# Attention with a computed position bias and a gated MLP on one core: another order of the bias groups, with three attention steps among the last ones

## The chip, the cores and the metric

The kernel runs on one core of one Trainium2 chip. The metric is device time in microseconds (us) of one execution; lower is better. The engines are TensorE (PE in the profile; PEld is its weight load), VectorE (DVE), ScalarE (ACT), GpSimd (POOL) and SyncE (SP), which here only issues transfers. Each works through its own instructions in the order in which the program emits them, and waits on semaphores for the others.

## What is computed

Attention over 4 batches, 8 heads, 576 positions and 64 dimensions per head, with a bias on the scores that a small network makes from the distance of two positions; then, on the 2304 resulting rows, a product with `w_in`, a rational function, and a product with `w_out`.

```python
psi_rel = np.log1p(np.abs(pos[:, None] - pos[None, :]))
psi_i = np.log1p(np.maximum(pos[:, None], 1.0))
h = np.maximum((psi_rel / psi_i)[..., None] @ w1 + b1, 0.0)
scores = scale * q @ k.T + (h @ w2).transpose(2, 0, 1)[None]
attn = softmax(scores); x = attn @ v
h = x @ w_in
P = a[0] + a[1] * h + a[2] * h**2 + a[3] * h**3
Q = 1.0 + abs(b[0]) * abs(h) + abs(b[1]) * h**2
out = (P / (Q + 1e-6)) @ w_out
```

## The kernel before

The program has three parts, and the change lies in the first and in the seam to the second.

**Bias groups** (L564 to L655). The bias of a row of positions depends on the distance alone, so it is made as tables in DRAM. There are 36 groups `n` of 16 positions. For a group, `relu(n)` (L596) makes four rows of hidden units, each as long as the largest distance that occurs, `dist(n)` (576 elements for the first and the last group, 304 in the middle); VectorE makes them, and in every fourth group ScalarE makes one of the four (`ENG`, L587). They go into a ring of 14 slots, and run `LEAD` = 2 groups ahead. Four products on TensorE (L633) make the group's tile `pb` in PSUM, ScalarE evicts it in two instructions (L642) into one of five tiles `e`, and SP writes `e` to the table in DRAM (L647). Table `tab[g]` holds eight groups, the last one four. The loop goes over `n` in rising order, so the tables are finished in the order 0 to 4.

`load_bias(p, c)` (L242) loads table `c` for the pair of heads `p` into SBUF as three transfers (288, 256 and 32 KB; two of 144 KB for table 4). For the first pair it stands in the loop, two groups after a table is done; that of table 4 comes after the loop (L655).

**Attention** (L320 to L562). Sixteen units (a pair of heads, a batch) of five steps make 80 steps; step `c` of a unit takes 128 queries of both heads, step 4 the last 64 of both. `step_a(i)` (L495) emits, in this order: transfers for later steps; the score products of step `i` (L340); the rest of the exponentials of step `i - 1`; the transposes of step `i - 2` (L418) and their copies; some products with `v` (L451, L456); then on VectorE the reduction of step `i` (L351), which adds bias table `c` of the unit's pair and takes the row maximum, and the first exponential (L369) on ScalarE. A step's scores lie in one or two tiles of the PSUM pool `ps_sc`, which has two, so the scores of a step wait until the reduction of an earlier one has read its tile. The tiles `pb` come from the same pool. The transposes use two tiles of the pool `ps_tp`. The last `EARLY` = 2 groups have steps 0 and 1 among them (L653); the other steps follow after L655.

**Weight jobs.** The weights of the second part are split into two halves by 20 jobs in the background of attention: two loads of 512 KB (`wx`, `wy`, L127 and L128), five VectorE and one ScalarE instructions, two stores. `run_jobs` (L486), called at the end of a step, emits as many of their VectorE instructions as `JOB_OPS` says (1, 2, 2, 1, 1 by the step), and every transfer that comes before the next of them. With 0, as in step 2, it emits the loads of the first two jobs alone; from step 3 on the first job's VectorE instructions follow.

SP issues nearly all transfers on one queue, in the order emitted. Before the bias groups, a prologue on VectorE (L576 to L586) scales the constants; ScalarE's row uses the table `pts` that it leaves.

The lines that set the seam:

```python
if k == 2 and g:
    load_bias(0, g - 1)
if n >= NG - EARLY:
    step_a(n - NG + EARLY)
...
load_bias(0, 4)
```

Of the kernel before, what the change touches and what calls it, by code (L numbers as in the profile page):

```python
# [16 lines left out]
P = 128  # L17
# [17 lines left out]
def tile_attn_moe(  # L35
# [185 lines left out]
    with tc.manual_schedule():  # L221
# [3 lines left out]
        with ExitStack() as actx:  # L225
# [260 lines left out]
            def run_jobs(n):  # L486
                while bg and (n > 0 or bg[0][0] != "dve"):
                    kind, fn = bg.pop(0)
                    if kind == "act":
                        actq.append(fn)  # L490
                    else:
                        fn()
                    n -= kind == "dve"

            def step_a(i):  # L495
                def ok(d):
                    return 0 <= i - d < NS

                if i < NS:
                    u, c = steps[i]  # L500
                    if c == 1 and u + 1 < NU:
                        load_qk(u + 1)
                    if c == 2 and u + 1 < NU:
                        load_v(u + 1)
                    g = {(0, 4): 0, (1, 1): 1, (1, 4): 2, (2, 1): 3, (2, 4): 4}.get((units[u][1], c))
                    if g is not None and units[u][0] + 1 < NP:
                        load_bias(units[u][0] + 1, g)
                    if i == NS - 7:
                        load_x(0, 0)
                first = []  # L510
                if NS - 4 <= i < NS:
                    first = split_x(0, i - NS + 4)
                if first:
                    first[0]()
                    later.append(first[1])
                while len(later) > (1 if i < NS - 1 else 0):
                    later.pop(0)()
                if ok(0):
                    e_qk(i)
                if ok(1):  # L520
                    for j in heads(i - 1)[1:]:
                        e_exp(i - 1, j)
                run_act()
                if ok(TL):
                    hs = heads(i - TL)
                    for j in hs:
                        for o, x in e_tp(i - TL, j):
                            A.copy(out=o, in_=x)  # L528
                    tails, fin = e_tail(i - TL)
                for _ in range(PV_KEYS[(i - TL) % 5] if i < NS + TL else len(fill)):  # L530
                    if fill:
                        e_pv(*fill.pop(0))
                if ok(0):
                    for j in heads(i):
                        e_ttr(i, j)
                    e_exp(i, heads(i)[0])
                if ok(1) and steps[i - 1][1] == 4:
                    e_recip(steps[i - 1][0])
                if ok(TL):
                    for o, x in tails:  # L540
                        A.copy(out=o, in_=x)
                    if fin:
                        fin()
                    u2, c2 = steps[i - TL]
                    if c2 in (1, 4):
                        fill.extend((u2, c2 // 4, kc) for kc in range(5))
                if 0 <= i - NS < 2:
                    mm1(0, i - NS)
                if i == NS:
                    w_carve(3)  # L550
                    w_load(KH - 2, 0)
                    w_load(KH - 1, 0)
                if i == NS + 1:
                    load_x(1, 1)
                u2, c2 = divmod(i - TL, 5)
                if c2 == 0 and 1 < u2 <= NU:
                    e_norm(u2 - 2)
                if c2 == 0 and 0 < u2 <= NU:
                    load_rb(u2 - 1)
                if i >= 2:  # L560
                    run_jobs(JOB_OPS[c2] if i >= 3 else 0)
                e_pvout()  # L562

            with ExitStack() as bctx:  # L564
# [8 lines left out]
                nc.sync.dma_start(out=lts, in_=ltab)  # L573
                nc.scalar.dma_start(out=cs, in_=cst)
                load_qk(0, nc.scalar)
                V.tensor_scalar(out=lts, in0=lts, scalar1=w1s, scalar2=None, op0=ALU.mult)  # L576
                V.tensor_scalar(out=pts, in0=pts, scalar1=b1s, scalar2=None, op0=ALU.mult)
                V.tensor_scalar(out=nts, in0=pts, scalar1=-1.0, scalar2=None, op0=ALU.mult)
                V.tensor_scalar(out=w28, in0=cs[:, 8 + 5 * NG:], scalar1=8.0, scalar2=None, op0=ALU.mult)
                V.memset(qc, 1.0 + 1e-6)  # L580
                V.memset(wmin, -8.0 * 0x38000000)
                pc = ps_tp.tile([P, 512], F32, tag="tp", name="pc")
                T.matmul(pc[:, 0:1], w28, b1s, start=True, stop=True)
                V.memset(c8, 0.0)
                V.tensor_copy(out=c8[:, 0:1], in_=pc[:, 0:1])
                V.tensor_copy(out=c8[0:96, 1:2], in_=pc[0:96, 0:1])  # L586
                ENG = ["DDDA" if n % 4 == 0 else "DDDD" for n in range(NG)]  # L587

                def dist(n):
                    return max(NROW * n + NROW, S - NROW * n)  # L590

                rows = {}
                LEAD, EARLY = 2, 2
                nring = [0]

                def relu(n):  # L596
                    for c, e in enumerate(ENG[n]):
                        r = ring[nring[0] % len(ring)][:, :dist(n)]
                        nring[0] += 1
                        m = 4 * n + c  # L600
                        if e == "A":
                            A.activation(out=r, in_=lts[:, :dist(n)], func=AF.Relu, bias=pts[:, m:m + 1])
                        else:
                            V.tensor_scalar(
                                out=r, in0=lts[:, :dist(n)], scalar1=nts[:, m:m + 1], scalar2=None,
                                op0=ALU.max,
                            )
                        rows[n, c] = r
# [9 lines left out]
                    after[15 + f] = [lambda f=f: [w_load(f, z) for z in range(2)]]  # L618
                bg = in_order(bg, after)

                for n in range(LEAD):
                    relu(n)
                for n in range(NG):
                    if n == 4:
                        load_v(0)
                    if n + LEAD < NG:
                        relu(n + LEAD)
                    ps = ps_sc.tile([P, 2, 512], F32, tag="sc", name=f"pb{n}")
                    ps = ps.rearrange("p a s -> p (a s)")
                    for s0 in range(0, dist(n), 512):  # L630
                        s1 = min(s0 + 512, dist(n))
                        for c in range(4):
# [15 lines left out]
                        out=tab[g][NROW * k:NROW * k + NROW, :, x0:x0 + EW].rearrange("r h x -> (r h) x"),  # L648
                        in_=e,
                    )  # L650
                    if k == 2 and g:
                        load_bias(0, g - 1)
                    if n >= NG - EARLY:  # L653
                        step_a(n - NG + EARLY)
                load_bias(0, 4)  # L655
                A.activation(out=babs, in_=abs_[:, 4:6], func=AF.Abs)

            wpool = ctx.enter_context(
# [273 lines left out]
```

## Time and profile before

| | |
|---|---|
| median of 3 runs | 746.05 us (744.64 to 746.75) |
| the profiled execution | 745.69 us |
| its span, from the first to the last instruction | 743.9 us |
| TensorE busy | 723.1 us (97%) |
| VectorE, ScalarE, GpSimd busy | 581.7 us (78%), 514.9 us (69%), 184.5 us (25%) |

The profile comes from one execution. Times in it are microseconds from the first instruction, names are those of the program with the number of the buffer left out, and the line is that of the kernel. A busy time includes the overlap of pipelined instructions; idle time is put down to what released the engine. TensorE's clock has two levels, 2.4 GHz (1.00 in the windows) and 1.2 GHz (0.50).

### The profile page before, as it was taken

The page shows a single profiled execution, that of the slowest core. Times are in us where ns is not written, and L with a number is a line of the kernel's source. Part 1 is how long each engine was busy: PE and PEld are TensorE (multiplying, and loading weights), DVE is VectorE, ACT ScalarE, POOL GpSimd, SP SyncE. Part 2 cuts the span into 40 slices and gives each one's busy share as a digit, 9 for nine tenths or more (in the row PEclk, how much of TensorE's full clock was granted, in tenths as well). Part 3 has the DMA queues.
Part 4 walks back from the last instruction along what each step waited for, and adds up shares of the span by engine and source line. Part 5 has one row for each costly group of instructions (what it writes and reads, how often), then busy time and mean ns, then how long its engine had stood idle before and what let it go on. Part 6 is the DMA issues. An engine that isn't in the chain of part 4 may idle for free.

```text
span 743.9 us, 12201 instructions
## 1 busy us (share of the span) xinstructions
PE 723.1 (97%) x4210; PEld 550.7 (74%) x4210; DVE 581.7 (78%) x979; ACT 514.9 (69%) x965; POOL 184.5 (25%) x106
## 2 busy tenths in 40 slices
PE   6898999999999999999999999999999999999997
PEld 2235666665666666668889989998899989998896
DVE  7995566666676667546999999999997869787766
ACT  5987788887888787877575766667675665556552
POOL 0000000000000000003444445454554345434442
PEclk9999999999999999999999999999999999999999
DMA  4878797788988899637433344547952123031121
GB/s 140 300 285 279 237 291 268 224 269 285 317 261 284 271 283 297 206 89 236 153 128 127 128 151 140 172 166 240 306 185 85 54 75 126 3 128 47 39 86 42
DMA packets 107421, 137.67 MB, mean 185 GB/s; under 512 B 17104, under 2 KB 66528, under 8 KB 107360
## 3 DMA queue, kind: packets, MB, share of 16 engines
q1 hardware_dynamic: 106768, 136.11, 55.9%
q8 instruction: 33, 0.54, 0.3%
q10 hardware_dynamic: 592, 0.78, 0.3%
q14 instruction: 28, 0.23, 0.1%
HBM read 94.96 MB, written 41.90 MB: 184 GB/s over the span
## 4 chain that ended last, share of the span: by engine, by line
PE 86%; DMA 5%; DVE 3%; SPq 2%; ACT 2%; issue 1%; POOL 0%; DVEq 0%; ACTq 0%; POOLq 0%
PE o L767 25%; PE h L315 24%; PE sc L340 11%; PE pv L451 9%; PE tp L418 9%; PE pb L633 4%; PE pv L456 3%; DMA wy<-in_w_in_dram 2%; ACT e L642 2%; DMA wy<-in_w_out_dram 1%; PE pv L433 1%; DMA k<-in_kt_dram 1%; DMA tab<-e 1%; DMA cst<-in_cst_dram 0%; DVE m L722 0%
## 5 line engine op out<-in xcount | busy, mean ns | idle before, releaser
L697 POOL TENSOR_TENSOR u<-u,w 128x768 f32<-128x768 f32 x48 | 96.7, 2015 | 475.2 <-DMA xr<-xd 338.6
L351 DVE CUSTOM_DVE_ANT_0 s<-sc,bias 128x576 f32<-128x576 f32 x144 | 104.0, 755 | 76.4 <-PE sc L340 74.1
L369 ACT ACTIVATE p<-s,m 128x576 f32<-128x576 f32 x144 | 113.2, 786 | 3.4 <-DVE m L351 3.1
L528 ACT COPY ptm<-tp 128x512 f32<-128x512 f32 x144 | 78.2, 588 | 52.6 <-PE tp L418 52.0
L694 ACT ACTIVATE w<-h 128x768 f32<-128x768 f32 x48 | 39.0, 813 | 101.6 <-PE h L315 99.0
L736 POOL TENSOR_TENSOR gl<-m,r 128x768 fp32r<-128x768 f32 x47 | 87.1, 1854 | 72.5 <-DVE m L729 72.5
L315 PE MATMUL h<-xh,wg 128*128 128x384 f32 x384 | 101.8, 336 | 0.0
L340 PE MATMUL sc<-k,q 64*128 64x288 f32 x512 | 82.6, 430 | 4.3 <-DVE m L351 2.6
L418 PEld LDWEIGHTS tp<-ident,p 128*128 128x128 f32 x576 | 63.1, 141 | 26.7 <-issue 11.5
L451 PE MATMUL pv<-ptm,v 128*64 128x320 f32 (+1 forms) x512 | 80.4, 425 | 0.0
L418 PE MATMUL tp<-ident,p 128*128 128x128 f32 x576 | 79.8, 280 | 0.0
L767 PE MATMUL o<-wg,gh 128*128 128x512 f32 x288 | 79.0, 391 | 0.0
L340 PEld LDWEIGHTS sc<-k,q 64*128 64x128 f32 x512 | 45.7, 187 | 37.3 <-issue 7.9
L701 ACT ACTIVATE r<-u,qc 128x768 f32<-128x768 f32 x48 | 45.1, 940 | 37.5 <-POOL u L697 37.3
L315 PEld LDWEIGHTS h<-xh,wg 128*128 128x128 f32 x384 | 69.7, 188 | 1.1
L722 DVE SCALAR_TENSOR_TENSOR m<-u,qc,gh 128x768 f32<-128x768 f32 x48 | 66.0, 1375 | 5.4 <-DVE gh L715 0.5
L705 DVE TENSOR_TENSOR t<-t,h 128x768 f32<-128x768 f32 x48 | 45.5, 948 | 26.7 <-ACT t L696 15.8
L315 PE MATMUL h<-xh,wih 128*128 128x384 f32 x192 | 65.0, 338 | 0.9 <-DVE t L708 0.9
L315 PE MATMUL h<-xl,wih 128*128 128x384 f32 x192 | 64.7, 337 | 0.2 <-DVE xl L301 0.2
L315 PE MATMUL h<-xh,wil 128*128 128x384 f32 x192 | 64.7, 337 | 0.0
L315 PE MATMUL h<-xl,wg 128*128 128x384 f32 x192 | 64.4, 335 | 0.0
L715 DVE SCALAR_TENSOR_TENSOR gh<-t,cst,r 128x768 fp32r<-128x768 f32 x48 | 56.5, 1176 | 8.2 <-ACT r L702 5.8
(77 smaller groups left out, 1343.4 us busy)
## 6 DMA issues: line engine op xcount, KB each, us to landing
tab<-e SPq DMA_DIRECT2D x36, 295.5 KB, 3.5
wx<-in_w_in_dram SPq DMA_DIRECT2D x16, 512.0 KB, 5.5
wy<-in_w_in_dram SPq DMA_DIRECT2D x16, 512.0 KB, 6.0
wx<-in_w_out_dram SPq DMA_DIRECT2D x16, 512.0 KB, 4.7
wy<-in_w_out_dram SPq DMA_DIRECT2D x16, 512.0 KB, 5.7
ws<-wh SPq DMA_DIRECT2D x32, 256.0 KB, 5.6
ws<-wl SPq DMA_DIRECT2D x32, 256.0 KB, 4.8
wg<-ws SPq DMA_DIRECT2D x32, 256.0 KB, 5.3
```

Of the source, the lines that this page charges most:

```text
L315: T.matmul(hps[s][:, j, :TT], w[:, k, sl], x[:, k, :], start=(k == 0 and z == 0), stop=(k == KD - 1 and z == 2),)
L340: T.matmul(sc[i, j][:, a, :SH], l, k[r, o + a * SH:o + (a + 1) * SH], start=True, stop=True,)
L351: V.tensor_tensor_reduce(out=t.rearrange("p (a s) -> p a s", a=2), in0=sc.pop((i, j))[:, :, :SH], in1=bias[p][:, idx, :].rearrange("p (a s ...
L369: A.activation(out=prob[i][:, z * S:z * S + S], in_=t, func=AF.Exp, bias=m, scale=-1.0, accum_out=ssum[u][:, k:k + 1],)
L418: T.transpose(ps[:, kc, :], prob[i][:, k0:k0 + P], ident)
L451: T.matmul(ps[64 * j:64 * j + 64, :w], v[:, kc, 64 * j:64 * j + 64], ptm[u, hf][:, kc, j, :w], start=(kc == 0), stop=False,)
L528: A.copy(out=o, in_=x)
L697: G.tensor_tensor(out=u, in0=u, in1=w, op=ALU.mult)
L715: V.scalar_tensor_tensor(out=hi, in0=rt[s, "t"], scalar=abs_[:, 0:1], in1=rt[s, "r0"], op0=ALU.add, op1=ALU.mult,)
L722: V.scalar_tensor_tensor(out=m, in0=rt[s, "u"], scalar=qc, in1=rt[s, "gh"].bitcast(F32), op0=ALU.add, op1=ALU.mult,)
L736: eng.tensor_tensor(out=lo, in0=rt[s, "m"], in1=rt[s, "r0"], op=ALU.mult)
L767: T.matmul(po[n, c], l[:, j, c * P:(c + 1) * P], r[fp][:, j, :], start=(first and x is a), stop=(last and x is z),)
```

## The change

Six edits. The loop runs over `order`: groups 0 to 15, 32 to 35, 16 to 31. The loads of the finished tables stand at places of a table `done`, and the one after the loop is that of table 3. Groups 24 to 31, the last eight, take their PSUM tile from `ps_tp`. `EARLY` is 3. The prologue leaves two instructions on VectorE; the others go to ScalarE and GpSimd, with a table `bts` of its own for ScalarE's rows. The first job's VectorE instructions start with step 5 instead of step 3.

```diff
@@ -558,7 +558,7 @@
                 if c2 == 0 and 0 < u2 <= NU:
                     load_rb(u2 - 1)
                 if i >= 2:
-                    run_jobs(JOB_OPS[c2] if i >= 3 else 0)
+                    run_jobs(JOB_OPS[c2] if i >= 5 else 0)
                 e_pvout()
 
             with ExitStack() as bctx:
@@ -573,24 +573,27 @@
                 nc.sync.dma_start(out=lts, in_=ltab)
                 nc.scalar.dma_start(out=cs, in_=cst)
                 load_qk(0, nc.scalar)
+                bts = tpool.tile([P, NG * 4], F32, tag="bts", name="bts")
+                G.memset(qc, 1.0 + 1e-6)
+                G.memset(wmin, -8.0 * 0x38000000)
+                G.memset(c8, 0.0)
+                V.tensor_scalar(
+                    out=nts, in0=pts, scalar1=b1s, scalar2=-1.0, op0=ALU.mult, op1=ALU.mult
+                )
                 V.tensor_scalar(out=lts, in0=lts, scalar1=w1s, scalar2=None, op0=ALU.mult)
-                V.tensor_scalar(out=pts, in0=pts, scalar1=b1s, scalar2=None, op0=ALU.mult)
-                V.tensor_scalar(out=nts, in0=pts, scalar1=-1.0, scalar2=None, op0=ALU.mult)
-                V.tensor_scalar(out=w28, in0=cs[:, 8 + 5 * NG:], scalar1=8.0, scalar2=None, op0=ALU.mult)
-                V.memset(qc, 1.0 + 1e-6)
-                V.memset(wmin, -8.0 * 0x38000000)
+                A.activation(out=w28, in_=cs[:, 8 + 5 * NG:], func=AF.Identity, scale=8.0)
+                A.activation(out=bts, in_=pts, func=AF.Identity, scale=b1s)
                 pc = ps_tp.tile([P, 512], F32, tag="tp", name="pc")
                 T.matmul(pc[:, 0:1], w28, b1s, start=True, stop=True)
-                V.memset(c8, 0.0)
-                V.tensor_copy(out=c8[:, 0:1], in_=pc[:, 0:1])
-                V.tensor_copy(out=c8[0:96, 1:2], in_=pc[0:96, 0:1])
+                A.copy(out=c8[:, 0:1], in_=pc[:, 0:1])
+                A.copy(out=c8[0:96, 1:2], in_=pc[0:96, 0:1])
                 ENG = ["DDDA" if n % 4 == 0 else "DDDD" for n in range(NG)]
 
                 def dist(n):
                     return max(NROW * n + NROW, S - NROW * n)
 
                 rows = {}
-                LEAD, EARLY = 2, 2
+                LEAD, EARLY = 2, 3
                 nring = [0]
 
                 def relu(n):
@@ -599,7 +602,7 @@
                         nring[0] += 1
                         m = 4 * n + c
                         if e == "A":
-                            A.activation(out=r, in_=lts[:, :dist(n)], func=AF.Relu, bias=pts[:, m:m + 1])
+                            A.activation(out=r, in_=lts[:, :dist(n)], func=AF.Relu, bias=bts[:, m:m + 1])
                         else:
                             V.tensor_scalar(
                                 out=r, in0=lts[:, :dist(n)], scalar1=nts[:, m:m + 1], scalar2=None,
@@ -618,15 +621,20 @@
                     after[15 + f] = [lambda f=f: [w_load(f, z) for z in range(2)]]
                 bg = in_order(bg, after)
 
-                for n in range(LEAD):
+                order = [*range(16), *range(32, NG), *range(16, 32)]
+                done = {10: 0, 18: 1, 22: 4, 30: 2}
+                for n in order[:LEAD]:
                     relu(n)
-                for n in range(NG):
-                    if n == 4:
+                for y, n in enumerate(order):
+                    if y == 4:
                         load_v(0)
-                    if n + LEAD < NG:
-                        relu(n + LEAD)
-                    ps = ps_sc.tile([P, 2, 512], F32, tag="sc", name=f"pb{n}")
-                    ps = ps.rearrange("p a s -> p (a s)")
+                    if y + LEAD < NG:
+                        relu(order[y + LEAD])
+                    if 24 <= n < 32:
+                        ps = ps_tp.tile([P, 512], F32, tag="tp", name=f"pb{n}")
+                    else:
+                        ps = ps_sc.tile([P, 2, 512], F32, tag="sc", name=f"pb{n}")
+                        ps = ps.rearrange("p a s -> p (a s)")
                     for s0 in range(0, dist(n), 512):
                         s1 = min(s0 + 512, dist(n))
                         for c in range(4):
@@ -648,11 +656,11 @@
                         out=tab[g][NROW * k:NROW * k + NROW, :, x0:x0 + EW].rearrange("r h x -> (r h) x"),
                         in_=e,
                     )
-                    if k == 2 and g:
-                        load_bias(0, g - 1)
-                    if n >= NG - EARLY:
-                        step_a(n - NG + EARLY)
-                load_bias(0, 4)
+                    if y in done:
+                        load_bias(0, done[y])
+                    if y >= NG - EARLY:
+                        step_a(y - NG + EARLY)
+                load_bias(0, 3)
                 A.activation(out=babs, in_=abs_[:, 4:6], func=AF.Abs)
 
             wpool = ctx.enter_context(
```

Three places show what this does to the queues. In the rows below a tile's first number is the group, the unit or the step (`sc3_1`: step 3, second head), the last one a running number.

SP's queue, where the bias groups end. Before, from the last table write (group 35) on: `q1`, `k1`, `qdg1` and `v1` are the second unit's, `bias0` the first pair's bias, `wx`/`wy` the weight loads of the first two jobs.

```order
L647 DMA tab4_71<-e35_674 128x591
L261 DMA q1_678<-in_qt_dram 128x512
L262 DMA k1_679<-in_kt_dram 128x640
L265 DMA qdg1_111<-in_qt_dram 64x64 x2
L253 DMA bias0_317<-tab4_71 64x576 x2
L271 DMA v1_718<-in_vp_dram 128x4x128
L274 DMA vdg1_108<-in_vp_dram 64x64 x2
L127 DMA wx0_0_754<-in_w_in_dram 128x4x256
L128 DMA wy0_0_755<-in_w_in_dram 128x4x512
L127 DMA wx0_1_758<-in_w_out_dram 128x1024
L128 DMA wy0_1_759<-in_w_out_dram 128x2048
```

Of the change, from the last write but one on:

```order
L655 DMA tab3_70<-e30_665 128x591
L261 DMA q1_669<-in_qt_dram 128x512
L262 DMA k1_670<-in_kt_dram 128x640
L265 DMA qdg1_111<-in_qt_dram 64x64 x2
L655 DMA tab3_70<-e31_695 128x591
L271 DMA v1_699<-in_vp_dram 128x4x128
L274 DMA vdg1_108<-in_vp_dram 64x64 x2
L127 DMA wx0_0_735<-in_w_in_dram 128x4x256
L128 DMA wy0_0_736<-in_w_in_dram 128x4x512
L127 DMA wx0_1_739<-in_w_out_dram 128x1024
L128 DMA wy0_1_740<-in_w_out_dram 128x2048
L248 DMA bias0_318<-tab3_70 128x576
```

The last load of the first pair's bias stood ahead of `v1` and the four weight loads; now the last load, that of table 3, stands behind them.

TensorE's queue, where the bias groups end. Before, from group 34 on (`pb` are the groups' products, `sc` the scores):

```order
L633 MATMUL pb34_634<-ring2_124,w28_62 32x512 x4
L633 MATMUL pb34_634<-ring2_124,w28_62 32x48 x4
L340 MATMUL sc0_0_650<-k0_130,q0_129 128x288
L340 MATMUL sc0_1_651<-k0_130,q0_129 128x288
L340 MATMUL sc0_0_650<-k0_130,q0_129 128x288
L340 MATMUL sc0_1_651<-k0_130,q0_129 128x288
L633 MATMUL pb35_665<-ring_123,w28_62 32x512 x4
L633 MATMUL pb35_665<-ring_123,w28_62 32x64 x4
L340 MATMUL sc1_0_684<-k0_130,q0_129 128x288
L340 MATMUL sc1_1_685<-k0_130,q0_129 128x288
L340 MATMUL sc1_0_684<-k0_130,q0_129 128x288
```

Of the change, from group 29 on:

```order
L641 MATMUL pb29_636<-ring_123,w28_62 32x480 x3
L641 MATMUL pb29_636<-ring2_124,w28_62 32x480
L340 MATMUL sc0_0_645<-k0_130,q0_129 128x288
L340 MATMUL sc0_1_646<-k0_130,q0_129 128x288
L340 MATMUL sc0_0_645<-k0_130,q0_129 128x288
L340 MATMUL sc0_1_646<-k0_130,q0_129 128x288
L641 MATMUL pb30_660<-ring2_124,w28_62 32x496 x4
L340 MATMUL sc1_0_675<-k0_130,q0_129 128x288
L340 MATMUL sc1_1_676<-k0_130,q0_129 128x288
L340 MATMUL sc1_0_675<-k0_130,q0_129 128x288
L340 MATMUL sc1_1_676<-k0_130,q0_129 128x288
L641 MATMUL pb31_690<-ring_123,w28_62 32x512 x4
```

The scores of step 0 stood between the last two groups; now those of step 0, 1 and 2 stand behind groups 29, 30 and 31, the last three.

VectorE's queue at the first weight job. Before, from step 3's reductions on (`s2` and `m` are what a reduction writes, `wk`, `wm`, `wh` the job's):

```order
L351 ISA s2_3_0_782,m3_0_783<-sc3_0_762,bias0_317 128x576
L351 ISA m3_0_783 128x1
L351 ISA s2_3_1_785,m3_1_786<-sc3_1_763,bias0_317 128x576
L351 ISA m3_1_786 128x1
L139 TENSOR_SCALAR wk0_0_791<-wx0_0_754 128x512
L147 TENSOR_SCALAR wm0_0_793<-wy0_0_755 128x512
L351 ISA s2_4_2_823,m4_2_824<-sc4_2_799,bias0_317 128x576
L351 ISA m4_2_824 128x1
L152 SCALAR_TENSOR_TENSOR wh0_0_803<-wx0_0_754,wh0_0_803 128x512
L158 TENSOR_SCALAR wk0_0_791<-wh0_0_803 128x512
```

Of the change, from step 3's second reduction on:

```order
L351 ISA s2_3_1_786,m3_1_787<-sc3_1_764,bias0_318 128x576
L351 ISA m3_1_787 128x1
L351 ISA s2_4_2_818,m4_2_819<-sc4_2_796,bias0_318 128x576
L351 ISA m4_2_819 128x1
L351 ISA s2_5_0_847,m5_0_848<-sc5_0_824,bias0_318 128x576
L351 ISA m5_0_848 128x1
L351 ISA s2_5_1_850,m5_1_851<-sc5_1_825,bias0_318 128x576
L351 ISA m5_1_851 128x1
L376 TENSOR_SCALAR sum0_658<-sum0_658 128x9
L377 RECIPROCAL sum0_658<-sum0_658 128x9
L139 TENSOR_SCALAR wk0_0_859<-wx0_0_735 128x512
```

The job's first two instructions stood between the reductions of steps 3 and 4; now one stands behind those of step 5.

## Rows read from the trace of the kernel before

**Rows 1.** Page, part 4: the chain that ended last, shares by engine

```profile
PE 86%; DMA 5%; DVE 3%; SPq 2%; ACT 2%; issue 1%; POOL 0%; DVEq 0%; ACTq 0%; POOLq 0%
```

**Rows 2.** The chain, in order of time: start us, us, what

```profile
90.53 1.17 PE sc L340 x8
...
107.47 1.17 PE sc L340 x8
```

**Rows 3.** Timeline of the start: start, duration, engine, line [idle before <-releaser]

```profile
4.28 0.52 DVE L576 TENSOR_SCALAR lts<-lts,cst 128x576 f32<-128x576 f32 x1 [4.28 <-DMA cst<-in_cst_dram]
...
5.04 0.24 DVE L578 TENSOR_SCALAR nts<-cst 128x144 f32<-128x144 f32 x1
5.04 0.78 ACT L602 ACTIVATE ring<-lts,cst 128x576 f32<-128x576 f32 x1 [3.03 <-DVE cst L577]
...
6.23 18.93 DVE L604 TENSOR_SCALAR ring<-lts,nts 128x576 f32<-128x576 f32 x50
...
9.84 1.08 ACT L642 ACTIVATE e<-pb,c,cst 128x576 f32<-128x576 f32 x2 [4.02 <-PE pb L633]
```

**Rows 4.** Timeline, where the bias groups end

```profile
24.75 29.94 DVE L604 TENSOR_SCALAR ring<-lts,nts 128x368 f32<-128x368 f32 x86
...
56.19 0.76 DVE L351 CUSTOM_DVE_ANT_0 s<-sc,bias 128x576 f32<-128x576 f32 x1 [1.50 <-PE sc L340]
...
56.99 0.78 ACT L369 ACTIVATE p<-s,m 128x576 f32<-128x576 f32 x1 [1.66 <-DVE m L351]
...
57.67 0.18 ACT L369 ACTIVATION_READ_ACCUMULATOR p<-s,m 128x1 f32 x1
...
58.30 1.08 ACT L642 ACTIVATE e<-pb,c,cst 128x16 f32<-128x16 f32 x2 [0.45 <-ACT p L369]
```

**Rows 5.** Timeline, steps 4, 5 and 9

```profile
66.35 1.14 PE L340 MATMUL sc<-k,qdg 128*128 128x288 f32 x4
...
69.27 0.43 DVE L139 TENSOR_SCALAR wk<-wx 128x512 uint32<-128x512 uint32 x1 [2.42 <-DMA wx<-in_w_in_dram]
...
71.93 1.23 PE L340 MATMUL sc<-k,q 64*128 64x288 f32 x6 [2.21 <-DVE m L351]
...
87.83 1.13 PE L340 MATMUL sc<-k,qdg 128*128 128x288 f32 x4
```

**Rows 6.** Windows: length; busy PE, PEld, DVE, ACT, POOL; PEclk; DMA share; GB/s

```profile
70.00:71.00 1.00, 0.00 (x0) 0.00 (x0) 0.22 (x1) 1.00 (x3) 0.00 (x0) 1.00 1.03 419
...
73.00:74.00 1.00, 1.00 (x8) 0.90 (x8) 1.00 (x3) 0.21 (x1) 0.00 (x0) 0.83 0.96 338
74.00:75.00 1.00, 1.00 (x6) 0.67 (x6) 0.97 (x5) 0.77 (x2) 0.00 (x0) 0.50 0.69 127
...
77.00:78.00 1.00, 1.00 (x9) 0.51 (x7) 0.00 (x0) 0.00 (x0) 0.00 (x0) 0.96 1.03 362
```

**Rows 7.** SP's queue, 59 to 69 us: DMA issues

```profile
59.41 0.32 SPq L647 DMA_DIRECT2D tab<-e  x1
...
62.01 1.18 SPq L253 DMA_DIRECT2D bias<-tab  x2
63.24 0.59 SPq L271 DMA_DIRECT2D v<-in_vp_dram  x1
...
65.06 0.58 SPq L127 DMA_DIRECT2D wx<-in_w_in_dram  x1
...
67.33 0.39 SPq L248 DMA_DIRECT2D bias<-tab  x1
...
68.44 0.43 SPq L250 DMA_DIRECT2D bias<-tab  x1
```

**Rows 8.** DMA issues, median us to landing: whole span, then 67.3 to 69 us

```profile
tab<-e SPq DMA_DIRECT2D x36, 295.5 KB, 3.5
...
bias<-tab SPq DMA_DIRECT2D x1, 32.0 KB, 6.6
```

**Rows 9.** Timeline, step 35's score product

```profile
175.87 1.24 PE L340 MATMUL sc<-k,q 64*128 64x288 f32 x8 [0.61 <-DMA k<-in_kt_dram]
```

## Prediction

> **What bounds the kernel now.** I read the chain that ended last first: TensorE holds 86% of it, so over most of the span only TensorE's own work counts [rows 1]. Attention runs in 16 units of five steps, and from the third unit on a unit takes 107.47 - 90.53 = 16.94 us of it, back to back [rows 2]. What comes after the tenth step is therefore fixed work as long as nothing starves TensorE, and the change is worth what it does to one moment: the first score product of step 10, at 90.53 us now [rows 2].
>
> The timeline ahead of that moment shows two other bounds. First VectorE: its 135 row instructions (36 groups of four, nine of them on ScalarE) run without a gap from 6.23 us to 24.75 + 29.94 = 54.69 us [rows 3, 4]. Then a stall: at 69.27 VectorE has sat 2.42 us for the first weight load, because the first weight job stands ahead of step 4's score reduction in its queue, and at 71.93 TensorE has sat 2.21 us for that reduction [rows 5]. TensorE's granted clock pays too: it falls in the window at 73, is 0.50 (the lower level, 1.2 GHz) at 74, and is back at 0.96 in the window at 77 [rows 6].
>
> What that stall costs is read from a repetition. From step 4's score product to step 10's it took 90.53 - 66.35 = 24.18 us; the same piece of program one unit later (step 9's to step 15's) took 107.47 - 87.83 = 19.64 us [rows 2, 5]. So **4.5 us** are lost: 2.2 waiting, some 1.65 by half a clock over about 3.3 us (73.7 to 77.0, read from the mean clocks), the rest because step 5's score product was cut in two.
>
> **The change, part by part.**
>
> *Shorter prologue.* VectorE starts at 4.28 when the constants land, and its rows at 6.23 [rows 3]. Left for it now are one instruction like that of 5.04 (0.24 us) and one like that of 4.28 (0.52): rows from about 5.05, **1.2 us** earlier. What moved to ScalarE (two activations, two copies of a column with the small product ahead of them) held VectorE from 5.19 on for about 1.0 us; I allow 1.4 on ScalarE, to 5.7, and then its own row of group 0, in before at 5.04. The cover is ScalarE's idle time: before, it waited 4.02 us for TensorE until the first eviction at 9.84 [rows 3]. Without that cover the gain shrinks to nothing, not below: bounds -1.2 and 0; I take -1.2, since the constants, which release the first instruction, don't move. The three memsets that went to GpSimd lie beside the load of the constants.
>
> *Group order.* The same 36 groups make the same rows, so VectorE's total stays, and it ends near 53.5. Groups 32 to 35, the widest, now stand in the middle. Nothing is gained there.
>
> *Other PSUM tiles, three steps.* Now step 0's scores sit in their PSUM before the rows are done, and the first reduction runs at 53.5 instead of 56.19 [rows 4]. From there ScalarE sets the pace, with durations of [rows 4]: exponential (57.67 + 0.18 - 56.99 = 0.86 with its accumulator read) from 53.5 + 0.80 = 54.3 to 55.2; eviction of group 30 (1.08) to 56.2; two exponentials to 57.9; eviction of group 31, now the last, to **59.0**. Step 2's scores and transposes run beside it, and step 3's score product starts near 59.75. Up to here the change is ahead.
>
> *The last bias piece.* Step 3's reduction reads table 3, whose last rows are now those of group 31, and its load comes after the whole loop; three steps are in the loop now, so it stands behind step 2's issues: v and four weight loads of 512 KB. In SP's queue: last table write at 59.0, 0.3; then v, before 63.24 to 65.06, 1.8 us; weight loads from **61.1**, four issues, before 65.06 to 67.33, 2.3 us; bias from **63.4** [rows 7]. The write has over 4 us to land by then, and the median of such writes is 3.5 [rows 8]. So its own table doesn't delay it; what stands ahead in the transfers does. Before, step 4's loads for the next pair of heads stood at exactly this place, behind the same four loads, and had the same shape: their 32 KB rest, issued at 68.44, took 6.6 us to land, 75.04 [rows 7, 8]. That is 10.0 us after the first weight load was issued. The two pieces behind the first have 288 KB together, 0.7 us at the 419 GB/s of the window at 70 [rows 6], so the first, of 288 KB, landed some 9.2 us after it. So now: 61.1 + 9.2 = **70.3** for what step 3's first reduction needs, 71.1 for its second. The reduction takes 0.76 [rows 4]; step 4's score product, which needs its PSUM, starts at 71.05 instead of 66.35: **+4.7 us**. Queued behind the waiting reduction on VectorE are all of steps 3 to 5, behind step 4's score product on TensorE everything else. TensorE runs dry near 62.3, after step 1's transposes, and idles 8.7 us.
>
> The rows speak for a queue that is worked off in order. Bounds for the landing: 2.6 us after issue, as if nothing stood ahead (the write issued at 59.41 had to land before the load of 62.01) [rows 7], and 10.0 us after the first weight load. I take the copy of the same situation. The Trainium skill speaks against it in part (DMA: Bandwidth & Descriptors, section Queues, rings and completion order): each transfer engine takes up a queue's descriptors in order, but completion is not first in, first out over the transfers one engine issued. By that rule the bias could overtake, a rival below; the trace shows no sign of it, with 6.6 us for 32 KB.
>
> *Later first weight job.* It is consumed two steps later, after step 5's reductions; its load has landed by then. The **4.5 us** of the old stall go. The weight work ends two steps later, still ahead of attention's end by the order of the queues, and VectorE has room. The weight loads meet the k loads at other places; one such meeting costs 0.61 us now [rows 9]. It may vanish or come twice: 0.6 either way, taken as nothing.
>
> *The clock.* After 2.2 us of idling it fell, 1.8 us after TensorE was at work again, and was back 77.0 - 71.93 = 5.1 us after that restart [rows 5, 6]. After 8.7 us it will be down when step 4's scores start. If it comes back as late after the restart, half of 5.1 us is lost: **+2.5 us**. Bounds: 1.65 as before, and 3.3, twice as much.
>
> **Sum:** +4.7 - 4.5 + 2.5 = +2.7 us at step 10. All that the prologue won is inside the 4.7: without it that term would be 5.9. The profiled execution took 745.69 us (its span is 743.9), so it would take 748.4; the median of the runs shown is 0.36 higher, which gives 748.75, in round numbers **748.7 us**. A difference of 0.3% (2.2 us) is about what a measurement of this kernel can tell from no change.
>
> **Rivals.**
>
> *The prologue gives nothing* (VectorE waits for ScalarE's row or for free row slots). For it: ScalarE's first row, at 5.04 now, comes later. Against: TensorE, not ScalarE, holds up the first eviction. All later points move by 1.2: 749.9.
>
> *The idling costs less*, within 0.3%: the bias lands 1 us earlier, or the clock is back as soon as before. For it: the sum is a small difference of large terms. 4.7 - 4.5 + 1.65 = +1.85, or 0.85 with a landing 1 us earlier as well: about 747.4.
>
> *The bias overtakes the weights*, and the change wins. Issued at 63.4 and landed 2.6 us later, its first piece is there at 66.0, step 4's scores start at 66.75, +0.4; with 1.65 for the clock 0.4 - 4.5 + 1.65 = -2.45: about 743.6. It is faster by 0.3% from a landing before some 66.2 on. Against it stand the 6.6 us of the 32 KB. The rule of the Trainium skill named above would allow it.
>
> **Chances.** Slower by over 0.3%: the forecast 0.41 and the lost prologue 0.09, together 0.50. Within 0.3%: 0.38. Faster: 0.12, which holds the overtaking. The unknown costs spread the likeliest case by about -1 (clock at its lower bound) to +2 (prologue lost, or clock at its upper bound): its own range is 747.7 to 750.7. For 8 in 10 the whole reaches down to the overtaking and up a little beyond the prologue's loss: 743.5 to 751.0.
>
> **What would show it.** Right: rows on VectorE from about 5.05 and ended near 53.5; last table write near 59; step 3's first reduction at about 70, its wait ended by a transfer of the bias; TensorE without work from 62 to 71, then a low clock for some 5 us; the weight job without a wait; step 10's scores near 93. Wrong: step 3's reduction before 66, or no fall of the clock, or a start of steady work later than 95 because another load (k of a later unit) comes late.

## The result and the profile after

| | before | after |
|---|---|---|
| median | 745.59 us (744.64 to 746.75, 4 runs) | 755.88 us (755.17 to 758.52, 4 runs) |
| ratio after / before | | 1.0123 (95%: 1.0099 to 1.0146) |
| span of the profiled execution | 743.9 us | 753.4 us |

The changed kernel is 1.2% slower. Of the 9.5 us between the two spans, 2.55 are there at step 10's first score product, where the forecast had 2.7. The other 7.0 come later, where it had none.

The page of the kernel after, part 1, first row: TensorE's work is what it was (4210 products, busy for 723.2 us against 723.1), so what was lost is waiting and clock.

```profile
PE 723.2 (96%) x4210; PEld 552.2 (73%) x4210; DVE 581.9 (77%) x972; ACT 515.3 (68%) x969; POOL 184.0 (24%) x109
```

Timeline of VectorE after, at the start, at the first reduction and at step 3's (they answer to [rows 3 to 5]):

```profile
4.71 0.29 DVE L580 TENSOR_SCALAR nts<-cst 128x144 f32<-128x144 f32 x1 [4.71 <-DMA cst<-in_cst_dram]
...
5.47 1.80 DVE L607 TENSOR_SCALAR ring<-lts,nts 128x576 f32<-128x576 f32 x4
...
53.86 0.76 DVE L351 CUSTOM_DVE_ANT_0 s<-sc,bias 128x576 f32<-128x576 f32 x1
...
71.03 0.76 DVE L351 CUSTOM_DVE_ANT_0 s<-sc,bias 128x576 f32<-128x576 f32 x1 [10.71 <-DMA bias<-tab]
```

SP's queue after, from the last table write on (to [rows 7]):

```profile
59.12 0.53 SPq L655 DMA_DIRECT2D tab<-e  x1
...
61.41 0.59 SPq L127 DMA_DIRECT2D wx<-in_w_in_dram  x1
...
63.61 0.85 SPq L248 DMA_DIRECT2D bias<-tab  x1
```

Timeline of TensorE after, step 4's and step 10's scores, then windows of 1 us (to [rows 5, 6]; the column before the last two is the granted clock):

```profile
71.90 2.26 PE L340 MATMUL sc<-k,qdg 128*128 128x288 f32 x4 [9.16 <-issue]
...
93.01 1.24 PE L340 MATMUL sc<-k,q 64*128 64x288 f32 x8
```

```profile
64.00:65.00 1.00, 0.00 (x0) 0.00 (x0) 0.00 (x0) 0.00 (x0) 0.00 (x0) 0.81 1.00 348
65.00:66.00 1.00, 0.00 (x0) 0.00 (x0) 0.00 (x0) 0.00 (x0) 0.00 (x0) 0.50 1.06 347
...
74.00:75.00 1.00, 1.00 (x7) 1.00 (x6) 0.70 (x2) 0.00 (x0) 0.00 (x0) 0.57 0.00 0
75.00:76.00 1.00, 1.00 (x10) 0.51 (x7) 0.06 (x2) 0.96 (x3) 0.00 (x0) 1.00 0.68 177
```

The reader sees the forecast chain: last table write at 59.1, weight loads from 61.4, the bias issued at 63.6 behind them and landed 7.4 us later, step 3's reduction at 71.0, TensorE idle for 9.2 us. The clock stands at 0.50 (1.2 GHz) from 65 to 74 and is back at 75, 3 us after TensorE's restart. The 2.55 us so near the forecast are partly luck: the bias cost 0.85 us more than forecast and the clock 1.0 us less.

Then the part that the forecast had left at nothing. Timeline of TensorE after, every wait of over 0.5 us from step 10 to the seam:

```profile
197.15 1.75 PE L340 MATMUL sc<-k,q 64*128 64x288 f32 x8 [2.39 <-DMA k<-in_kt_dram]
...
325.96 0.66 PE L418 MATMUL tp<-ident,p 128*128 128x128 f32 x4 [0.76 <-ACT ptm L528]
327.19 0.66 PE L418 MATMUL tp<-ident,p 128*128 128x128 f32 x4 [0.58 <-ACT ptl L541]
...
353.70 0.41 PE L315 MATMUL h<-xh,wih 128*128 128x384 f32 x1 [1.81 <-DVE t L716]
```

Windows of 4 us behind the first and the last of them:

```profile
196.00:200.00 4.00, 2.85 (x14) 2.09 (x15) 1.14 (x3) 0.02 (x1) 0.00 (x0) 0.72 0.45 144
200.00:204.00 4.00, 4.00 (x28) 2.55 (x26) 1.85 (x8) 2.94 (x8) 0.00 (x0) 0.86 0.88 244
...
352.00:356.00 4.00, 2.30 (x10) 2.33 (x11) 3.96 (x4) 3.71 (x6) 1.84 (x1) 0.84 0.90 263
356.00:360.00 4.00, 4.00 (x19) 3.91 (x18) 3.83 (x5) 1.81 (x3) 1.21 (x1) 0.73 0.94 278
```

Set against the kernel before at each unit's last score product, the lateness is 2.55 us through step 34, 1.87 at step 39 (the 0.61 us wait of [rows 9] at step 35 is gone), 5.90 from step 44 on (2.39 of wait at step 40 and 1.6 of low clock behind it), 7.53 at step 79 (the transposes wait for ScalarE's copies, which stood behind a cast of the attention rows `xr` that waited 2.96 us for its load; the table calls them the late copies), and 9.5 behind the seam to the second part (1.81 instead of 0.89 us of wait, and a clock of 0.84 and 0.73 in two windows).

Where the k of the late step stood in SP's queue. Before, for step 35 [rows 9], timeline:

```profile
167.63 0.44 SPq L219 DMA_DIRECT2D wol<-ws  x1
168.16 0.39 SPq L261 DMA_DIRECT2D q<-in_qt_dram  x1
169.23 0.33 SPq L262 DMA_DIRECT2D k<-in_kt_dram  x1
```

After, for step 40:

```profile
181.06 0.45 SPq L219 DMA_DIRECT2D wih<-ws  x1
...
183.65 0.65 SPq L219 DMA_DIRECT2D wol<-ws  x1
184.34 1.65 SPq L253 DMA_DIRECT2D bias<-tab  x2
186.63 0.39 SPq L127 DMA_DIRECT2D wx<-in_w_in_dram  x1
187.06 0.51 SPq L128 DMA_DIRECT2D wy<-in_w_in_dram  x1
187.80 0.34 SPq L261 DMA_DIRECT2D q<-in_qt_dram  x1
188.65 0.34 SPq L262 DMA_DIRECT2D k<-in_kt_dram  x1
```

The chain of waits says how long the transfers took, before and then after:

```profile
169.23 6.50 DMA k<-in_kt_dram
```

```profile
181.56 7.03 DMA wil<-ws
...
188.65 8.37 DMA k<-in_kt_dram
```

Before, the last of four weight halves stood right ahead of q and k. Now a bias piece (288 KB) and the next job's two 512-KB loads stand between the halves and k, which lands 8.37 us after its issue instead of 6.50.

### The profile page after: what moved, and what is told of

It reads as the page before. It is cut to its first block, busy times and chain, and to the rows that moved or that the text cites. A ratio compares the mean times of both kernels' runs of the same rounds, so it can differ in the third digit from the quotient of the medians.

```text
span 753.4 us, 12189 instructions
## 1 busy us (share of the span) xinstructions
PE 723.2 (96%) x4210; PEld 552.2 (73%) x4210; DVE 581.9 (77%) x972; ACT 515.3 (68%) x969; POOL 184.0 (24%) x109
## 4 chain that ended last, share of the span: by engine, by line
PE 82%; DVE 6%; DMA 6%; issue 3%; SPq 1%; ACT 1%; POOL 0%; DVEq 0%; ACTq 0%; POOLq 0%
PE o L775 25%; PE h L315 24%; PE sc L340 11%; PE tp L418 9%; PE pv L451 8%; DVE ring L607 3%; PE pv L456 2%; PE pb L641 2%; DMA k<-in_kt_dram 2%; DMA wy<-in_w_in_dram 1%; DMA wil<-ws 1%; PE pv L433 1%; DMA xr<-xd 1%; DMA rb<-rs 1%; ACT e L650 1%
## 5 line engine op out<-in xcount | busy, mean ns | idle before, releaser
L723 DVE SCALAR_TENSOR_TENSOR gh<-t,cst,r 128x768 fp32r<-128x768 f32 x48 | 58.1, 1211 | 8.1 <-ACT r L710 5.8
```

What stands on the lines that cost most here:

```text
L723: V.scalar_tensor_tensor(out=hi, in0=rt[s, "t"], scalar=abs_[:, 0:1], in1=rt[s, "r0"], op0=ALU.add, op1=ALU.mult,)
```

## The experiments

Theory A: the later first job moves the weight traffic by two steps against all other loads of attention, and that puts it ahead of k, of the attention rows and of the seam's loads. Theory B: the late waits come from the other edits, which make the first part end later. The table has what the profile of each run shows: starts of step 4's and step 10's scores on TensorE, its waits in us for k (with the step), for ScalarE's late copies and at the seam, the span, and the timed ratio to the kernel before. Starts are those of the timeline, where step 10's stands 0.08 us ahead of the chain's [rows 2].

| run | step 4 | step 10 | k | copies | seam | span | ratio (95%) |
|---|---|---|---|---|---|---|---|
| before | 66.35 | 90.45 | 0.61 (35) | - | 0.89 | 743.9 | 1 |
| e8: before, again | 67.91 | 88.96 | 1.23 (35) | - | 0.82 | 743.3 | |
| after | 71.90 | 93.01 | 2.39 (40) | 0.76, 0.58 | 1.81 | 753.4 | 1.0123 (1.0099 to 1.0146) |
| e12: after, again | 71.47 | 93.61 | 2.69 (40) | - | 1.76 | 751.9 | |
| e1: job at step 3 | 72.14 | 93.80 | 1.89 (35) | - | 1.88 | 750.1 | 1.0063 (1.0044 to 1.0083) |
| e2: before, job at step 5 | 66.35 | 85.93 | 1.11 (40) | 0.58, 0.58 | 2.07 | 742.9 | 0.9984 (0.9965 to 1.0004) |
| e3: bias ahead | 65.16 | 86.44 | 1.30 (40) | 0.31, 0.58 | 1.99 | 743.9 | 1.0004 (0.9985 to 1.0023) |
| e4: bias ahead, catch-up | 65.71 | 87.04 | 0.52 (35), 0.30 | - | 2.12 | 742.5 | 0.9962 (0.9949 to 0.9976) |
| e5: catch-up | 71.48 | 93.18 | 0.66 (35) | - | 2.06 | 748.4 | 1.0046 (1.003 to 1.0062) |
| e6: k early | 71.83 | 93.01 | - | - | 2.04 | 748.2 | 1.0051 (1.0033 to 1.007) |
| e7: bias by ScalarE | 68.09 | 90.54 | 1.62 (40) | 2.21, 0.44 | 1.67 | 751.8 | 1.0034 (1.001 to 1.0058) |
| e9: ahead, catch-up, k | 65.42 | 86.69 | - | - | 2.17 | 742.5 | 0.9969 (0.9957 to 0.9981) |
| e10: old prologue | 73.46 | 95.83 | 1.18 (40) | 0.57 | 1.47 | 751.4 | 1.0088 (1.0065 to 1.011) |
| e11: before, catch-up, k | 66.32 | 85.90 | - | - | 1.75 | 740.0 | 0.9929 (0.9913 to 0.9946) |

**e1, the job at step 3 again.**

```diff
-                    run_jobs(JOB_OPS[c2] if i >= 5 else 0)
+                    run_jobs(JOB_OPS[c2] if i >= 3 else 0)
```

> The changed kernel with the job threshold back at step 3. Theory A (the threshold, by moving the weight traffic two steps against the loads of k, of the attention rows and of the reciprocals, cost the 7 us behind step 10): step 10's scores stay near 93, the waits for k at step 40 and for the late copies go, about 748.3 us. Theory B (the other edits, which end the first part later and in another order, brought those waits): they stay, about 755.5 us.

751.9 us, between the two. The wait at step 40 and the late copies go, as A says; in their place k is late at step 35, by 1.89 us (the clock stays at 1.00). So the threshold decides which step's k is late, but not alone how late it is: the same place cost 0.61 us before.

**e2, the kernel before with that edit alone** on its own.

```diff
-                    run_jobs(JOB_OPS[c2] if i >= 3 else 0)
+                    run_jobs(JOB_OPS[c2] if i >= 5 else 0)
```

> The kernel before with the job threshold at step 5 alone. The stall ahead of step 4's reduction goes, step 10's scores near 86 instead of 90.5. Theory A: the late waits of some 7 us appear, about 748 us in all. Theory B: they don't, about 741 us.

744.67 us. The old stall is gone (step 10's scores 4.5 us earlier), and step 40's wait for k and the late copies appear in a kernel that has nothing else of the change: A. With the seam they give back 3.5 of the 4.5 us, half of what A expected for the late waits, and the time can't be told from that of the kernel before.

**e3, the last bias piece ahead of step 2's loads** (changed kernel).

```diff
-                done = {10: 0, 18: 1, 22: 4, 30: 2}
+                done = {10: 0, 18: 1, 22: 4, 30: 2, 35: 3}
...
-                load_bias(0, 3)
```

> The changed kernel with the last bias piece issued ahead of step 2's loads. Both theories: step 3's reduction no later than 66.5 instead of 71, step 10's scores near 88 instead of 93. Theory A: the late waits stay, about 750.5 us. Theory B, if the lateness of the bias brought them: they go, about 743 us. If the bias lands as late as before (what is issued ahead is not what holds it), step 10 stays at 93.

747.06 us. The issue and what it ends, timeline of SP and of VectorE in this run:

```profile
61.35 0.33 SPq L248 DMA_DIRECT2D bias<-tab  x1
```

```profile
64.30 0.76 DVE L351 CUSTOM_DVE_ANT_0 s<-sc,bias 128x576 f32<-128x576 f32 x1 [4.47 <-DMA bias<-tab]
```

With no weight load ahead, the piece lands 2.95 us after its issue instead of 7.4, and step 10's scores come 6.6 us earlier than in the changed kernel. The waits at step 40 and for the copies stay at their places, so the late bias isn't what puts them there, against B; they are smaller.

**e4 and e5, the jobs caught up**, with the bias ahead (e4) and behind (e5):

```diff
-                    run_jobs(JOB_OPS[c2] if i >= 5 else 0)
+                    run_jobs(JOB_OPS[c2] + (i in (6, 7, 10, 11)) if i >= 5 else 0)
```

> The changed kernel with the last bias piece ahead of step 2's loads and one weight instruction more in each of steps 6, 7, 10 and 11, so that from step 12 on the weight traffic stands against the other loads where it stood in the kernel before. Theory A: step 10's scores near 88 and no late waits, about 743 us, under the kernel before. Theory B: as without the four instructions moved.

> The changed kernel, bias piece still behind the weight loads, with one weight instruction more in each of steps 6, 7, 10 and 11, so that from step 12 on the weight traffic stands where it stood in the kernel before. The first part stays as it is in the changed kernel: step 10's scores near 93. Theory A (the place of the weight traffic alone makes the late waits): no wait of 2 us for k at step 40 and none for the late copies, the late part costs at most 2 us more than before, about 749.5 us. If the lateness of the first part itself makes the late waits: 755 us.

743.93 and 750.48 us. SP's queue in e5, around the loads of k for steps 35 and 40, and then TensorE's timeline at step 35:

```profile
170.99 0.43 SPq L219 DMA_DIRECT2D wol<-ws  x1
171.52 0.38 SPq L261 DMA_DIRECT2D q<-in_qt_dram  x1
172.59 0.33 SPq L262 DMA_DIRECT2D k<-in_kt_dram  x1
...
182.84 0.53 SPq L127 DMA_DIRECT2D wx<-in_w_in_dram  x1
183.41 0.51 SPq L128 DMA_DIRECT2D wy<-in_w_in_dram  x1
...
187.05 1.30 SPq L262 DMA_DIRECT2D k<-in_kt_dram  x1
```

```profile
178.64 1.24 PE L340 MATMUL sc<-k,q 64*128 64x288 f32 x8 [0.66 <-DMA k<-in_kt_dram]
```

The weight halves stand right ahead of step 35's k again, and the wait there is 0.66 us, about the 0.61 of before the change [rows 9]. From step 10 to step 79 e5 keeps its lateness at 2.7 to 2.8 us, where the changed kernel goes from 2.55 to 7.53. Four VectorE instructions at other steps are worth 1.0123 - 1.0046, some 5.7 us of 746. Theory A holds for k and, as far as they appear, for the late copies: ScalarE waits 1.6 to 4.4 us for `xr` in every run with the shift but e12, and at most 1.0 us without it. It doesn't hold for the seam, whose wait stays at 2.1 us in e4 and e5.

**e6, q and k issued a step earlier** (changed kernel).

```diff
-                    if c == 1 and u + 1 < NU:
+                    if c == (u == 0) and u + 1 < NU:
                         load_qk(u + 1)
```

> The changed kernel with q and k of the next unit issued one step earlier (from the second unit on), ahead of the weight halves that stand before them now. If k is late because of its place in the queue, the wait of 2.39 us at step 40 and the low clock behind it go: 4.0 us of the 9.5, about 752 us; the late copies and the seam stay. If k is late for another reason: 755.5 us.

751.17 us: no wait for k is left at either step. SP's queue at the k of step 40:

```profile
185.27 0.37 SPq L262 DMA_DIRECT2D k<-in_kt_dram  x1
...
187.92 0.39 SPq L127 DMA_DIRECT2D wx<-in_w_in_dram  x1
```

The edit puts k ahead of the two 512-KB loads; the four halves (to 182.5) and the bias piece still stand ahead of it, other than the expectation says. So an issue 3.4 us earlier and ahead of the two loads is enough to end the wait; which of the two counts, this run doesn't separate. The gain is more than expected (1.0123 to 1.0051, some 5.4 us), because TensorE's waits for the late copies are gone too: ScalarE still waits 1.63 us for `xr`, but only 0.3 us of that is left at step 79.

**e7, the last bias piece from ScalarE's queue** (changed kernel).

```diff
-                load_bias(0, 3)
+                load_bias(0, 3, nc.scalar)
```

> The changed kernel with the last bias piece issued from ScalarE's queue at the same moment, behind the same four weight loads in time. If the order of one issuing queue holds the bias back, its first piece lands about 3 us after issue, step 3's reduction near 66.5, step 10's scores near 88, 749 to 751 us. If the transfers already handed out hold it, whatever queue it comes from, step 3's reduction stays near 71 and the time near 755.5 us.

748.49 us. Its issue, and step 3's reduction, in the timelines of ScalarE and VectorE:

```profile
61.80 0.34 ACTq L248 DMA_DIRECT2D bias<-tab  x1
```

```profile
67.22 0.76 DVE L351 CUSTOM_DVE_ANT_0 s<-sc,bias 128x576 f32<-128x576 f32 x1 [7.41 <-DMA bias<-tab]
```

It lands 5.4 us after issue, between the 2.95 of e3 and the 7.4 of the changed kernel. It is no clean test: it was issued 1.8 us earlier than there, with two of the four weight loads after it. Neither answer is right by itself. The profile is also of the slowest of its 11 runs (753.63 us): 5.9 us of it are lost at the late copies, with waits of 2.21 and 0.44 us and the clock down to 0.50 behind them. The Trainium skill (DMA: Bandwidth & Descriptors, section Queues, rings and completion order) says that a transfer engine serves the queues that have work for it in turn, which would fit a piece that shares the transfer engines with the weights instead of standing behind all of them; no run here shows the turns.

**e8 and e12, both kernels profiled again.**

> The kernel before, profiled once more, to see how much the waits for loads vary from one execution to the next. If they are fixed by the program: 0.61 us for k at step 35, 0.89 us at the first products of the second part, no other wait for a load above 0.3 us. If chance has a hand in them, waits of another size or at another place.

> The changed kernel profiled once more. If the late waits are fixed by the program: 2.4 us for k at step 40, 0.6 to 0.8 twice for the late copies, 1.8 at the first products of the second part. If chance sets their size, they stand at the same places with other sizes, and the time is between 754 and 758 us.

The places of the waits for k and at the seam are the same in both profiles of a kernel. The late copies are not fixed by the program: e12 (753.65 us) has neither them nor a wait for `xr`. The sizes vary. In e8 (745.15 us) the old stall was 0.67 us in place of the 2.21 of [rows 5], timeline of TensorE:

```profile
72.02 1.23 PE L340 MATMUL sc<-k,q 64*128 64x288 f32 x6 [0.67 <-DVE m L351]
```

Behind it the clock stayed at 1.00. It had fallen earlier instead, windows of 1 us in e8:

```profile
63.00:64.00 1.00, 1.00 (x4) 0.29 (x3) 0.82 (x3) 0.00 (x0) 0.00 (x0) 0.50 0.82 170
...
73.00:74.00 1.00, 1.00 (x9) 0.81 (x8) 1.00 (x4) 0.20 (x2) 0.00 (x0) 1.00 1.00 355
```

That fall made step 4's scores 1.56 us later (67.91 against 66.35). The first job's load landed as early as before (its first instruction at 69.38, before at 69.27 [rows 5]) and the reduction behind the job came no later, so TensorE, which came to it later, waited less. From step 4 to step 10 it took 88.96 - 67.91 = 21.05 us, against 19.58 in e2, which has no stall: the stall cost 1.5 us here, not 4.5. Of the 3.0 us by which step 10 is later than in e2 (85.93), the other half is the early fall of the clock.

**e10, the changed kernel with the prologue of before** (that part of the change undone; its core):

```diff
-                V.tensor_scalar(
-                    out=nts, in0=pts, scalar1=b1s, scalar2=-1.0, op0=ALU.mult, op1=ALU.mult
-                )
...
-                A.activation(out=w28, in_=cs[:, 8 + 5 * NG:], func=AF.Identity, scale=8.0)
-                A.activation(out=bts, in_=pts, func=AF.Identity, scale=b1s)
+                V.tensor_scalar(out=pts, in0=pts, scalar1=b1s, scalar2=None, op0=ALU.mult)
+                V.tensor_scalar(out=nts, in0=pts, scalar1=-1.0, scalar2=None, op0=ALU.mult)
+                V.tensor_scalar(out=w28, in0=cs[:, 8 + 5 * NG:], scalar1=8.0, scalar2=None, op0=ALU.mult)
```

> The changed kernel with the prologue of before. The rows start 0.8 us later on VectorE, and everything up to step 4's scores by as much: step 3's reduction near 71.8, step 10's scores near 93.8. If the late waits don't change, about 756.5 us; if the prologue gives nothing at the first reduction, step 10 stays at 93.0.

752.94 us. The first reduction stands at 54.62, where all profiles with the new prologue but the first have it at 53.3 to 53.4: 1.3 us. Step 10's scores are 2.2 to 2.8 us later than in the two profiles of the changed kernel. Yet the total isn't more; the interval of its ratio overlaps with the changed kernel's. The waits behind step 10 are smaller here (1.18 us for k), so what the prologue wins is not seen at the end.

**e9 and e11, what is best.** e9 is e4 with e6's edit; e11 is the kernel before with e4's and e6's edits, without the new order, tiles, steps and prologue. e11 against the kernel before:

```diff
-                    if c == 1 and u + 1 < NU:
+                    if c == (u == 0) and u + 1 < NU:
...
-                    run_jobs(JOB_OPS[c2] if i >= 3 else 0)
+                    run_jobs(JOB_OPS[c2] + (i in (6, 7, 10, 11)) if i >= 5 else 0)
```

> The changed kernel with all three remedies: the last bias piece ahead of step 2's loads, one weight instruction more in each of steps 6, 7, 10 and 11, and q and k of the next unit issued one step earlier. Theory A: step 10's scores near 87, no wait for k, so some 0.6 us under the run with the first two remedies: about 743 us, below the kernel before by some 0.4 to 0.5%. If the late waits only move elsewhere: 745 us or more.

> The kernel before with the first job's VectorE instructions from step 5 on, one more in each of steps 6, 7, 10 and 11, and q and k issued one step earlier; the order of the groups, the PSUM tiles, the two early steps and the prologue are those of before. If the order of the groups and the third early step win nothing, this is the fastest: step 10's scores near 86, no wait for k or for the late copies, about 741.5 us. If they win something that the bias piece hid, it stays behind the run with all three remedies.

743.85 us (743.55 to 745.57) and **741.31 us** (740.53 to 741.88). e9 is not under e4, so moving k wins nothing there. e11 beats both kernels, 0.7% under the one before. Its TensorE at step 4 and step 10, and windows of 4 us between the two and at the seam:

```profile
66.32 1.14 PE L340 MATMUL sc<-k,qdg 128*128 128x288 f32 x4
...
85.90 1.24 PE L340 MATMUL sc<-k,q 64*128 64x288 f32 x8
```

```profile
70.00:74.00 4.00, 4.00 (x32) 2.70 (x31) 2.49 (x8) 4.00 (x11) 0.00 (x0) 1.00 1.03 405
...
344.00:348.00 4.00, 4.00 (x20) 3.23 (x18) 3.69 (x4) 3.43 (x4) 1.61 (x1) 1.00 0.96 294
```

From step 4 to step 10 it takes 19.58 us, the undisturbed 19.6, and the clock is 1.00 in every window of 4 us up to 736 us. e9's TensorE waits 3.20 us for the bias at step 4 and sees 0.50 from 66 to 69, so even with its piece ahead the new order of the groups loses 0.8 us at step 10 to the old one. From step 79 to the end e9 loses another 1.7: its wait at the seam is longer (2.17 against 1.75), and the clock is 0.81 and 0.77 in two windows of 4 us there, 1.00 in e11.

## Why the prediction was right and wrong

**The last bias piece: right.** "+4.7 us" was +5.55 at step 4's scores (71.90 against 66.35), and 5.1 to 5.8 in e1, e5, e6 and e12, which have the piece at the same place. In the changed kernel's first profile the constants landed 0.5 us later than in those (4.71 against 4.16 to 4.20), but that doesn't explain the spread. Every point of the chain, from the first reduction to step 3's, came within 0.9 us. e3 shows the cause, by undoing it: 6.7 us at step 4.

**The old stall: right for the profile it was read from.** "The 4.5 us of the old stall go": e2, which removes it alone, gains 4.52 at step 10. But in e8 the same stall costs 1.5 us, because step 4 came later and the clock didn't fall behind it, so the term hung on one profile.

**The clock: right in kind, its size spreads.** "+2.5 us" was 93.01 - 71.90 - 19.58 = 1.5 in the profile of the changed kernel, a little under its lower bound of 1.65; 2.6 in e12, 2.8 in e10.

**The prologue: right as a term, and the rival that it gives nothing fell at the first reduction.** 1.2 us forecast, 1.3 by e10 (0.8 in the changed kernel's first profile); at the end e10 shows none of it.

**The bias overtaking the weights: fell.** 7.4 us from issue to landing behind the weights, 2.95 without them ahead. The prediction leaned for this rival on the Trainium skill's sentence that completion is not first in, first out. The same section also says that the signal of a transfer's end lands only after every earlier write of that transfer engine, which speaks against the rival; the 7.4 us agree with that.

**The step that failed** is this: "The weight loads meet the k loads at other places; one such meeting costs 0.61 us now. It may vanish or come twice: 0.6 either way, taken as nothing." It priced the new meeting by the old one. The new one, at step 40, has a bias piece and two 512-KB loads between the four halves and k, and cost 2.39 us and 1.6 of clock, 4.0 in place of 0.7. Before, the k of step 40 stood behind two such loads and a bias piece without the halves, and didn't wait, and the k of step 35 stood right behind the halves; the shift put both ahead of one k. The step also looked at k alone: the attention rows came late as well (1.6 us). With it fell the sentence that what comes after the tenth step is fixed work. e2, e3, e7, e10 and e12 all have the wait at step 40 with the shift, e1, e4 and e5 don't; e4 and e5 show what undoing it alone is worth, 0.42% and 0.77%. The direction came out as forecast, slower, but by 10.3 us of the medians instead of 2.7, far outside the range.

**Open:** the size of the waits behind step 10, which a later first part seems to raise (2.4 and 2.7 us for k with the bias behind, 1.1 and 1.3 in e2 and e3; e10 with 1.18 speaks against it). And the seam: 1.5 to 2.2 us in every variant, 0.8 to 0.9 in both profiles of the kernel before. In the chain of waits of the changed kernel the last load of the reciprocals (`rb`) took 4.75 us there, in those two 2.80 and 3.11. e1, without the shift, and e2, with the shift alone, both have it, so neither the shift nor the rest is needed for it; its cause was not tried.

## What to carry to other kernels

When an edit shifts a stream of loads on a queue that others share, list for each load with a due time what stands ahead of it in the new order, in bytes, and price each new meeting by those bytes instead of by the old meeting; a shift that looks free is the first suspect. Issue the small load that a step waits for ahead of the bulk loads that nobody waits for yet, and keep the alignment of a stream that is already tuned when its start moves. Profile the kernel before twice: a stall read from one execution was a third as large in the next here. And look at the clock in windows of a few us: the page's 40 slices show 9 throughout for the kernel before and for e8, which both fell to 0.50 for some 3 us.

## What the runs showed of the hardware

What a wait of TensorE costs beyond itself didn't follow from its length alone. For k, 2.39 and 2.69 us were followed by a lower granted clock and 1.6 to 1.7 us more lost, while 0.66 to 1.89 us cost only themselves. At the seam, waits of 1.81 (changed kernel), 1.99 (e3) and 2.17 us (e9) were followed by a clock of some 0.7 to 0.8 in a window of 4 us, and waits of 1.47 to 2.12 us in the nine other profiles of changed programs left it at 1.00. At step 4, idling of 9.2 to 10.0 us cost TensorE 1.5 to 2.8 us beyond itself by step 10, 5.86 us (e7) cost 2.9, and 2.9 to 3.5 us (e3, e4, e9) cost 1.7 to 1.8.

Behind the same work the clock can fall in one execution and not in another. The two profiles of the kernel before have the same waits up to 62 us (0.58 and 0.39 us ahead of the scores at 59.44 and 61.07) and the same busy time; then the clock of one is 1.00 from 62 to 66, that of the other some 0.5 from 62 to 65. The same stall of this program cost 4.5 us in one profile and 1.5 in the other, and the wait for k at step 35 was 0.61 and 1.23 us. A term read from one execution carries that spread.
